# Polynomial-sketch attention followed by a sigmoid-gated feed-forward layer: other pieces for turning the first weight blocks into float32

## The chip, the cores and the metric

The kernel runs on one core of one Trainium2 chip. The metric is the device time of one execution in microseconds (us), lower is better. A difference under about 0.2% (0.6 us here) is not told from no change.

## What is computed

```
q, k, v: (4 batches, 4 heads, 1088 tokens, 32);  S1, S2: (8, 32)
phi(x) = outer product of S1 x and S2 x, flattened to 64 features
num = phi(q) @ (phi(k)^T v)      den = phi(q) . sum(phi(k)) + 1e-6
x = (num / den), heads side by side: 4352 tokens x 128
gate = sigmoid(x @ w_gate)       val = x @ w_val        # 128 x 1536 each
out = (gate * val) @ w_out                              # 1536 x 128
```

S1, S2 and the three weight matrices arrive as float64. The kernel gets their bits as pairs of 32-bit integers and makes float32 of them itself; the text calls this *narrowing*.

## The kernel before

**Feed-forward.** The 1536 hidden columns are 12 blocks of 128 (`NJ`), the 4352 tokens are chunks of 512. `w1` (line 345) computes one block of one chunk: two products into PSUM, gate and val (`wave`, line 357), which I call W0 to W11 in the first chunk; ScalarE takes the sigmoid of the gate (`sg`, line 365), and VectorE multiplies by val (`glu`, line 381). `w2` (line 307) multiplies that by the block's `w_out` and adds it up in PSUM (`moeout`, line 314) over the 12 blocks. A float32 product shows as two matmul instructions, so a `w1` is four and a `w2` two. `slot(group, n)` (line 395) issues n such steps in the order: `glu` of the last wave, `w2` of the wave before that, then the next `w1`.

**Attention** is issued between these steps by hand. For the first batch (batch 0) it comes in two parts of the queries, 512 and 576 columns (`q_chk`): part 0 must be done before W0, part 1 is done during chunk 0. For part 1, `turn_q(0, 1)` transposes the queries on VectorE (line 436), `qcomp` (line 593) multiplies them by the sketch (`cqps`, line 602), ScalarE copies the result out and sends it to DRAM, SyncE's queue brings it back spread over the partitions (`qp`, `bq`, line 627), `qmult` (line 653) multiplies the two on VectorE, and then `dn` (line 834) makes `dps` and `nps` on TensorE. Their result is divided on VectorE (lines 878 to 886), and this is what the second token chunk needs. Then batch 1 begins: `turn_k(1)`, `turn_q(1, 0)`, `turn_q(1, 1)` on VectorE, and `kps` and `cqps` on TensorE.

**Order.** The schedule is manual: on TensorE, VectorE, ScalarE and GpSimd instructions run in the order in which the program issues them. SyncE's queue issues its transfers in program order too.

**Narrowing** (`narrow`, line 83) is a generator with these steps for a part of the weights:

- step 0: GpSimd clamps the high words (`cap`, line 97), ScalarE scales the low words (`tail`, line 101);
- step 1: two VectorE instructions build the result's bits (`head`, line 105 from `cap`, and line 109 from `cap` and `head`);
- step 2: ScalarE squares `cap` (`square`, line 117, into a PSUM bank or in place in SBUF), GpSimd adds `tail` to `head` (line 118);
- step 3: VectorE writes the float32 part of `w_sb` from `square` and `head` (line 127).

`cap`, `tail` and `head` rotate over 6, 5 and 3 buffers. The parts are: gate and val of block 0; gate and val of block 1; `w_out` of blocks 0 and 1 together (these three are 256 wide, `narrow_01`); then for each block 2 to 11 gate, val and `w_out` together (384 wide, `narrow_w`). `w1` issues their steps inside the slots of chunk 0, after the sigmoid (lines 366 to 376). Blocks 10 and 11 keep `square` in SBUF, the others in PSUM.

**Loads.** Line 155 loads gate and val, line 168 `w_out` of two blocks at a time, all from SyncE's queue.

Of the kernel before, what the change touches and what calls it, by code (L numbers as in the profile page):

```python
# [8 lines left out]
F32 = mybir.dt.float32  # L9
I32 = mybir.dt.int32  # L10
# [10 lines left out]
def kernel(  # L21
# [30 lines left out]
    const = ctx.enter_context(tc.tile_pool(name="const", bufs=1))  # L52
    ld = ctx.enter_context(tc.tile_pool(name="ld", bufs=1))
    sbA = ctx.enter_context(tc.tile_pool(name="sbA", bufs=2))
    raw = ctx.enter_context(tc.tile_pool(name="raw", bufs=NJ // 2))
    sbN = ctx.enter_context(tc.tile_pool(name="sbN", bufs=1))
    sbG = ctx.enter_context(tc.tile_pool(name="sbG", bufs=6))

# [24 lines left out]
    def narrow(out, bits, eng, bank=None, copies=None):  # L83

        p, n, m = bits.shape[:3]
        lo, hi = bits[:, :, :, 0].bitcast(U32), bits[:, :, :, 1]

        def tmp(dt, tag, bufs):
            return sbN.tile([P, 3, P], dt, tag=tag, name=tag, bufs=bufs)[:p, :n, :m]

        cap, tail = tmp(I32, "cap", 6), tmp(I32, "tail", 5)
        eng.tensor_scalar(  # L97
            out=cap.bitcast(F32), in0=hi.bitcast(F32), scalar1=122880.0, scalar2=-122880.0,
            op0=ALU.min, op1=ALU.max,
        )  # L100
        nc.scalar.activation(out=tail, in_=lo, func=ACTF.Copy, scale=2.0**-29)  # L101
        yield

        head = tmp(I32, "head", 3)
        nc.vector.tensor_scalar(  # L105
            out=head, in0=cap, scalar1=3, scalar2=0x3FFFFFF8,
            op0=ALU.logical_shift_left, op1=ALU.bitwise_and,
        )
        nc.vector.scalar_tensor_tensor(  # L109
            out=head, in0=cap, scalar=-0x40000000, in1=head, op0=ALU.bitwise_and, op1=ALU.bitwise_or  # L110
        )
        yield
        square = cap.bitcast(F32)
        if bank:
            square = pso.tile([P, 512], F32, tag=bank, name="square")[:, : n * m]
            square = square.rearrange("p (n m) -> p n m", n=n)
        nc.scalar.activation(out=square, in_=cap.bitcast(F32), func=ACTF.Square)  # L117
        nc.gpsimd.tensor_tensor(out=head, in0=head, in1=tail, op=ALU.add)  # L118
        yield

        head = head.bitcast(F32)
        if copies:
            square, head = (
                bass.AP(tensor=x.tensor, offset=x.offset, ap=[list(x.ap[0]), [0, copies], [1, m]])
                for x in (square, head)
            )
        nc.vector.scalar_tensor_tensor(  # L127
            out=out, in0=square, scalar=1.265625 * 2.0**-30, in1=head, op0=ALU.is_ge, op1=MUL
        )
        yield  # L130
# [11 lines left out]
                nc.sync.dma_start(out=rows, in_=s_)  # L142


    w_sb = const.tile([P, 3, NJ, P], F32, tag="w_sb", name="w_sb")
    w_in = {}

    def load_w_in(j0, j1):
        cs = slice(j0 * P, j1 * P)
        n, jj = divmod(j0, 2)  # L150
        if wide and jj == 0:
            w_in[n] = raw.tile([P, 3, 2, P, 2], I32, tag="w_in", name="w_in")
        for i, src in enumerate((moe_w_gate, moe_w_val)):
            if wide:
                nc.sync.dma_start(  # L155
                    out=w_in[n][:, i, jj : jj + j1 - j0].rearrange("p j m w -> p (j m w)"),
                    in_=src[:, cs].bitcast(I32),
                )
            else:
                nc.sync.dma_start(  # L160
                    out=w_sb[:, i, j0:j1].rearrange("p j m -> p (j m)"), in_=src[:, cs]
                )

    def load_w_out(n):
        j0, j1 = 2 * n, 2 * n + 2
        cs = slice(j0 * P, j1 * P)
        src = moe_w_out[cs, :].bitcast(I32) if wide else moe_w_out[cs, :]
        nc.sync.dma_start(
            out=w_in[n][:, 2].rearrange("p j m w -> p j (m w)") if wide else w_sb[:, 2, j0:j1],
            in_=src.rearrange("(j p) m -> p j m", p=P),  # L170
        )

    narrowing = {}

    def narrow_w(j, step):
        if not 0 <= j < NJ:
            return
        n, jj = divmod(j, 2)
        if wide:
            if step == 0:  # L180
                narrowing[j] = narrow(
                    w_sb[:, :, j, :], w_in[n][:, :, jj], nc.gpsimd, "acc1" if j < NJ - 2 else None
                )
            next(narrowing[j])


    def narrow_01(part, step):
        if wide:
            if step == 0:
                i = (slice(0, 2), part) if part < 2 else (2, slice(0, 2))  # L190
                narrowing["01", part] = narrow(
                    w_sb[:, i[0], i[1]],
                    w_in[0][:, i[0], i[1]],
                    nc.gpsimd,
                    "acc0" if part else "acc1",
                )
            next(narrowing["01", part])


    def load_rows(src, b, t, parts=((0, T, nc.sync),)):  # L200
# [42 lines left out]
    load_w_in(0, 1)  # L243
    v_t[0] = load_v(0)
    load_w_in(1, 2)
    load_w_out(0)
    load_rows(q, 0, q_t[0], ((T0, T, nc.sync),))
    for n in range(1, NJ // 2):
        load_w_in(2 * n, 2 * n + 2)
        load_w_out(n)  # L250


    def warm(*cols):
# [53 lines left out]
    def w2(ci, j0, jn, g):  # L307
# [4 lines left out]
        for jj in range(jn):  # L312
            j = j0 + jj
            nc.tensor.matmul(  # L314
                out=moe["acc"][:, :tw],
                lhsT=w_sb[:, 2, j, :],
                rhs=g[:, jj, :tw],
                start=(j == 0),
                stop=(j == NJ - 1),
            )  # L320
        if j0 + jn == NJ:
# [6 lines left out]
            while c < t0 + tw:  # L328
# [13 lines left out]
                    )  # L342
                c += n * 32

    def w1():

        ci = moe["ci"]
        t0, tw = tok_chk[ci]
        jn = TCH // tw
        j0 = moe["w"] * jn  # L350
        wv = psm.tile([P, 2, TCH], F32, tag="wave", name="wave")

        tp = tw // 2 if ci == 0 and j0 == 0 else tw
        for o in range(0, tw, tp):
            for which in range(2):
                for jj in range(jn):
                    nc.tensor.matmul(  # L357
                        out=wv[:, which, jj * tw + o : jj * tw + o + tp],
                        lhsT=w_sb[:, which, j0 + jj, :],
                        rhs=xT[:, t0 + o : t0 + o + tp],  # L360
                        start=True,
                        stop=True,
                    )
        sg = sbG.tile([P, TCH], F32, tag="sg", name="sg", bufs=3)
        nc.scalar.activation(out=sg, in_=wv[:, 0], func=ACTF.Sigmoid)  # L365
        if ci == 0:
            if j0 == 1:
                narrow_01(2, 3)
            if 0 < j0 < NJ - 2:
                narrow_w(j0 + 1, 3)  # L370
            narrow_w(j0 + 2, 1)
            narrow_w(j0 + 2, 2)
            if j0 < 3:
                narrow_w(j0 + 3, 0)
            if j0 > 1:
                narrow_w(j0 + 4, 0)


        def glu():
            g = sbG.tile([P, TCH], F32, tag="g", name="g")  # L380
            nc.vector.tensor_tensor(out=g, in0=wv[:, 1], in1=sg, op=MUL)  # L381
            moe["todo"].append((ci, j0, jn, g.rearrange("p (j t) -> p j t", j=jn)))

        moe["gate"] = glu
        moe["w"] += 1
        if j0 + jn == NJ:
            moe["ci"] += 1
            moe["w"] = 0
# [38 lines left out]
            in_=k_t[b][:, t0:t1].rearrange("p t d -> p (t d)"),  # L427
        )

    def turn_q(b, n):  # L430
        if b >= B:
            return
        if n == 0:
            qT_of[b] = sbA.tile([P, TP, 2, 32], F32, tag="qT", name="qT", bufs=1)
        t0, tn = q_chk[n]
        nc.vector.transpose(  # L436
            out=qT_of[b][:, t0 : t0 + tn].rearrange("p t c s -> p (t c s)"),
            in_=q_t[b][:, 2 * t0 : 2 * (t0 + tn)].rearrange("p t d -> p (t d)"),
# [211 lines left out]
                        in_=bass.AP(tensor=d0.tensor, offset=offset, ap=[[8 * W1, 32]] + run),  # L650
                    )

    def qmult(b, n):
        q0 = half(QP[b], n)
        nc.vector.tensor_tensor(out=q0, in0=q0, in1=half(BQ[b], n), op=MUL)  # L655

    def kv0(j_list):
        if 0 not in KVZ:
# [34 lines left out]
            )  # L693

    def kvd(b):
        KVD[b] = sbA.tile([P, 2, 2, F], F32, tag="kvd", name="kvd")
        k0 = KVZ[b][:, : 2 * F]
        n = 2 if b > 0 else 1
        nc.scalar.copy(
# [211 lines left out]

    if wide:
        steps = narrow(s4, s_in, nc.vector, copies=4)
        for _ in range(3):
            next(steps)
    turn_k(0, 0, KBASE[2] + 1)
    if wide:
# [51 lines left out]
    mult10 = ab(None, (0, 1, 0), (psm, "wave"))  # L969
    for pi in range(2):  # L970
        outer(0, pi, NJK - 1, NJK, eng=nc.gpsimd)
    for part in range(2):
        narrow_01(part, 0)
    spread_z()
    warm(512)
    for pi in range(2):
# [6 lines left out]
    def rest(turn, rc, dT):  # L983
# [8 lines left out]
        narrow_01(0, 1)  # L992
        narrow_01(0, 2)
        ndt(0)

    divide = dn(0, 0, rest)
    warm(256)

    def head1():
        narrow_01(1, 1)  # L1000
        narrow_01(0, 3)
        narrow_01(1, 2)
        narrow_01(2, 0)
        narrow_w(2, 0)

    divide((0, 4), (4, 8), between=head1)
    narrow_01(1, 3)
    narrow_01(2, 1)
    narrow_01(2, 2)

    slot(None, 1)
    cq = {}
# [33 lines left out]
        kv(b, ZS[b])  # L1046
        kvd(b)

    slot(None, 1)
    turn_q(0, 1)  # L1050
    slot(None, 1)
    slot(q01, 6)
    qmult(0, 1)
    load_kq(1)
    slot(None, 1)
    slot(lambda: part01(lambda: narrow_w(NJ - 1, 3)), 1)
    slot(last01, 1)
    v_t[1] = load_v(1)
    for b in range(1, B):
# [60 lines left out]
```

## Time and profile before

| | us |
|---|---|
| median of 6 runs | 303.46 |
| lowest and highest | 303.32 and 303.99 |
| the profiled execution | 303.41 |
| its span, first to last instruction | 301.6 |
| mean granted TensorE clock | 0.999 of full speed |
| chunk 0, from the start of W0 to the start of its last `w2` | 15.01 to 51.13 |
| steady distance from one wave to the next in chunk 0 | 2.57 or 2.58 |

Times inside the execution are counted from the start of the span. A `timeline` line gives start, duration, engine, line, operation, output and inputs, shape; in brackets the engine's idle time before it and what ended it. The `PE` rows have modelled ends, so that a row can overlap the next one on the same engine.

### The profile page before, as it was taken

The page shows a single profiled execution, that of the slowest core. Times are in us where ns is not written, and L with a number is a line of the kernel's source. Part 1 is how long each engine was busy: PE and PEld are TensorE (multiplying, and loading weights), DVE is VectorE, ACT ScalarE, POOL GpSimd, SP SyncE. Part 2 cuts the span into 40 slices and gives each one's busy share as a digit, 9 for nine tenths or more (in the row PEclk, how much of TensorE's full clock was granted, in tenths as well). Part 3 has the DMA queues.
Part 4 walks back from the last instruction along what each step waited for, and adds up shares of the span by engine and source line. Part 5 has one row for each costly group of instructions (what it writes and reads, how often), then busy time and mean ns, then how long its engine had stood idle before and what let it go on. Part 6 is the DMA issues. An engine that isn't in the chain of part 4 may idle for free.

```text
span 301.6 us, 3642 instructions
## 1 busy us (share of the span) xinstructions
PE 294.5 (98%) x1363; PEld 137.2 (45%) x1363; DVE 154.7 (51%) x268; ACT 80.6 (27%) x150; POOL 33.0 (11%) x62
## 2 busy tenths in 40 slices
PE   8899999999999999999999999999999999999994
PEld 3444434453444444434444445344444444444683
DVE  6997789764635545383365444932232223222331
ACT  3556532222122222212232222122222222222220
POOL 1465550410000400000004000000000000000000
PEclk9999999999999999999999999999999999999999
DMA  7994340896011491360016900200020000100011
GB/s 222 348 339 112 93 141 9 200 238 181 39 17 18 139 228 30 71 193 0 0 28 162 223 17 2 36 2 0 0 33 2 0 0 12 25 0 0 9 28 19
DMA packets 30546, 24.24 MB, mean 80 GB/s; under 512 B 20480, under 2 KB 25728, under 8 KB 30528
## 3 DMA queue, kind: packets, MB, share of 16 engines
q1 hardware_dynamic: 27024, 16.15, 20.4%
q0 software_dynamic: 2592, 7.08, 10.2%
q10 hardware_dynamic: 912, 0.77, 1.0%
q8 instruction: 11, 0.18, 0.2%
q14 instruction: 7, 0.06, 0.1%
HBM read 20.73 MB, written 3.26 MB: 80 GB/s over the span
## 4 chain that ended last, share of the span: by engine, by line
PE 84%; DMA 6%; DVE 4%; POOL 2%; SPq 1%; issue 1%; ACT 0%; POOLq 0%; DVEq 0%
PE wave L357 52%; PE moeout L314 27%; DMA w_in<-in_moe_w_out_dram 2%; POOL head L118 2%; DMA kq<-in_q_dram 2%; PE nps L861 1%; DMA v<-in_v_dram 1%; DMA w_in<-in_moe_w_val_dram 1%; PE kvz L677 1%; DVE w_sb L127 1%; DVE head L109 1%; DVE qp L655 1%; DVE head L105 1%; PE kps L456 1%; SPq L155 0%
## 5 line engine op out<-in xcount | busy, mean ns | idle before, releaser
L357 PE MATMUL wave<-xT,w_sb 128*128 128x512 f32 (+1 forms) x436 | 191.6, 565 | 0.0
L381 DVE TENSOR_TENSOR g<-wave,sg 128x512 f32<-128x512 f32 x102 | 70.3, 689 | 131.0 <-ACT sg L365 130.7
L357 PEld LDWEIGHTS wave<-xT,w_sb 128*128 128x128 f32 x436 | 82.9, 190 | 93.0 <-issue 85.7
L365 ACT ACTIVATE sg<-wave 128x512 f32<-128x512 f32 x102 | 60.9, 597 | 197.8 <-PE wave L357 197.8
L314 PE MATMUL moeout<-g,w_sb 128*128 128x512 f32 (+1 forms) x216 | 105.2, 575 | 0.3 <-DVE w_sb L127 0.3
L314 PEld LDWEIGHTS moeout<-g,w_sb 128*128 128x128 f32 x216 | 39.9, 190 | 44.7 <-issue 39.1
L118 POOL TENSOR_TENSOR head<-head,tail 128x384 int32<-128x384 int32 (+2 forms) x14 | 13.4, 954 | 18.0 <-DVE head L109 14.9
L627 POOL DMA_DIRECT2D qp<-dq x6 | 3.5, 583 | 106.2 <-DMA dq<-cq 106.2
L535 DVE TENSOR_TENSOR kp<-kab 128x1152 f32<-128x1152 f32 (+2 forms) x10 | 10.5, 1070 | 0.0
L655 DVE TENSOR_TENSOR qp<-qp,bq 128x1152 f32<-128x1152 f32 (+1 forms) x7 | 9.0, 1288 | 0.0
L109 DVE SCALAR_TENSOR_TENSOR head<-cap,head 128x384 int32<-128x384 int32 (+2 forms) x14 | 7.5, 535 | 0.5
L127 DVE SCALAR_TENSOR_TENSOR w_sb<-square,head 128x384 f32<-128x384 f32 (+1 forms) x11 | 5.7, 518 | 3.9 <-POOL head L118 3.9
L258 PE MATMUL warm<-const-float32-1.0 128*128 128x512 f32 (+1 forms) x12 | 6.4, 653 | 0.8 <-PEq L1104 0.8
L324 DVE STREAM_TRANSPOSE o_sb<-moeout 128x512 f32<-128x512 f32 (+1 forms) x9 | 6.1, 679 | 1.4 <-PE moeout L314 1.3
L101 ACT ACTIVATE tail<-w_in 128x384 int32<-128x384 uint32 (+1 forms) x13 | 6.5, 522 | 0.9 <-DMA w_in<-in_moe_w_gate_dram 0.9
L627 POOL DMA_DIRECT2D bq<-dq x12 | 6.7, 574 | 0.5 <-issue 0.4
L97 POOL TENSOR_SCALAR cap<-w_in 128x384 f32<-128x384 f32 (+1 forms) x13 | 6.5, 505 | 0.0
L886 DVE TENSOR_TENSOR xT<-nps,rb 128x576 f32<-128x576 f32 (+2 forms) x9 | 5.9, 660 | 0.5
L861 PE MATMUL nps<-qp,nd 64*32 64x256 f32 (+1 forms) x128 | 5.5, 402 | 0.5 <-ACT nd L741 0.4
L436 DVE STREAM_TRANSPOSE qT<-kq 128x512 f32<-128x512 f32 (+1 forms) x8 | 5.7, 716 | 0.0
L117 ACT ACTIVATE square<-cap 128x384 f32<-128x384 f32 (+1 forms) x11 | 5.1, 463 | 1.9 <-DVE w_sb L127 1.7
L425 DVE STREAM_TRANSPOSE kT<-kq 128x1088 f32<-128x1088 f32 (+2 forms) x5 | 5.3, 1069 | 0.0
(89 smaller groups left out, 85.4 us busy)
## 6 DMA issues: line engine op xcount, KB each, us to landing
qp<-dq POOLq DMA_DIRECT2D x6, 576.0 KB, 7.5
bq<-dq POOLq DMA_DIRECT2D x12, 288.0 KB, 9.6
v<-in_v_dram SPq DMA_DIRECT2D x16, 144.0 KB, 4.3
kq<-in_k_dram SPq DMA_DIRECT2D x3, 544.0 KB, 4.2
kq<-in_q_dram SPq DMA_DIRECT2D x3, 544.0 KB, 5.2
w_in<-in_moe_w_out_dram SPq DMA_DIRECT2D x6, 256.0 KB, 6.2
w_in<-in_moe_w_gate_dram SPq DMA_DIRECT2D x5, 256.0 KB, 5.6
w_in<-in_moe_w_val_dram SPq DMA_DIRECT2D x5, 256.0 KB, 6.1
```

The lines of the kernel that those rows point to most:

```text
L97: eng.tensor_scalar(out=cap.bitcast(F32), in0=hi.bitcast(F32), scalar1=122880.0, scalar2=-122880.0, op0=ALU.min, op1=ALU.max,)
L109: nc.vector.scalar_tensor_tensor(out=head, in0=cap, scalar=-0x40000000, in1=head, op0=ALU.bitwise_and, op1=ALU.bitwise_or)
L118: nc.gpsimd.tensor_tensor(out=head, in0=head, in1=tail, op=ALU.add)
L127: nc.vector.scalar_tensor_tensor(out=out, in0=square, scalar=1.265625 * 2.0**-30, in1=head, op0=ALU.is_ge, op1=MUL)
L314: nc.tensor.matmul(out=moe["acc"][:, :tw], lhsT=w_sb[:, 2, j, :], rhs=g[:, jj, :tw], start=(j == 0), stop=(j == NJ - 1),)
L357: nc.tensor.matmul(out=wv[:, which, jj * tw + o : jj * tw + o + tp], lhsT=w_sb[:, which, j0 + jj, :], rhs=xT[:, t0 + o : t0 + o + tp], sta ...
L365: nc.scalar.activation(out=sg, in_=wv[:, 0], func=ACTF.Sigmoid)
L381: nc.vector.tensor_tensor(out=g, in0=wv[:, 1], in1=sg, op=MUL)
L535: eng.tensor_tensor(out=KP[b][:, pi, j0:j1].rearrange("p j m (i l) -> p (j m) i l", i=R), in0=bass.AP(tensor=a0.tensor, offset=a0.offset, ...
L627: get.dma_start(out=t[64 * c : 64 * c + 64 if i else P, n * H * W1 : (n + 1) * H * W1], in_=bass.AP(tensor=d0.tensor, offset=d0.offset, ap ...
L655: nc.vector.tensor_tensor(out=q0, in0=q0, in1=half(BQ[b], n), op=MUL)
L861: nc.tensor.matmul(out=t[32 * h : 32 * h + 32, c, :w], lhsT=ND[b][rows, 32 * h : 32 * h + 32], rhs=half(QP[b], n)[rows, 2 * (h % 2) + h // ...
```

## The change

- Gate and val of block 2 become a part of their own (256 wide, after those of blocks 0 and 1), and `w_out` of block 0 and of block 1 become parts of their own (128 wide).
- From then on the part j (3 to 11) is gate and val of block j with `w_out` of block j - 1 (384 wide); a part 12 is `w_out` of block 11 alone (128 wide). There are 15 parts of the weights instead of 13, over the same 36 x 128 columns.
- `narrow` gets one more yield, between its two `head` instructions, so that its steps are numbered 0 to 4.
- `square` stays in SBUF for parts 10, 11, 12 and for `w_out` of block 1.
- `turn_q(0, 1)`, one transposition of 576 columns before the second `glu`, becomes two of 320 and 256, issued inside the slots of W2 and W3 (`between`). The group `q01` (`cqps` and what follows) moves from before W3 to before W4.
- `w_out` is loaded as blocks 0, 1, 2, then (3, 4), (5, 6), (7, 8), (9, 10), 11: eight transfers instead of six.
- The tile `kvd` has one buffer instead of two; the raw words of each block pair have a tile of their own name; `w_sb` is laid out flat with one spare block, and `qmult` gets arguments that no call uses.

```diff
     def load_w_out(j0, j1):
+        src = moe_w_out[j0 * P : j1 * P, :]
+        to = w_sb[:, 2 * NJ + 1 + j0 : 2 * NJ + 1 + j1]
+        if wide:
+            n, jj = divmod(j0 + 1, 2)
+            to = w_in[n][:, 2 if n < NJ // 2 else 0, jj : jj + j1 - j0]
...
+    def narrow_w(part, *steps):
+        for step in steps if part in places else ():
             if step == 0:
+                at, bits, bank = places[part]
+                narrowing[part] = narrow(w_sb[:, at], bits, nc.gpsimd, bank)
+            next(narrowing[part])
+
+    places = {}
+    for j in range(NJ if wide else 0):
+        bits = w_in[j // 2][:, :, j % 2]
+        if j < 3:
+            at = slice(j, j + NJ + 1, NJ)
+            places["gv", j] = at, bits[:, :2], f"acc{1 - j % 2}"
+        else:
+            at = slice(j, j + 2 * NJ + 1, NJ)
+            places[j] = at, bits, "acc1" if j < NJ - 2 else None
+    if wide:
+        for j, bank in enumerate(("acc0", None)):
+            places["out", j] = (
+                slice(2 * NJ + 1 + j, 2 * NJ + 2 + j), w_in[j][:, 2, 1 - j : 2 - j], bank
+            )
+        places[NJ] = slice(3 * NJ, 3 * NJ + 1), w_in[NJ // 2][:, 0], None
...
-    load_w_out(0)
+    load_w_out(0, 1)
+    load_w_out(1, 2)
     load_rows(q, 0, q_t[0], ((T0, T, nc.sync),))
     for n in range(1, NJ // 2):
         load_w_in(2 * n, 2 * n + 2)
-        load_w_out(n)
+        if n == 1:
+            load_w_out(2, 3)
+        else:
+            load_w_out(2 * n - 1, 2 * n + 1)
+    load_w_out(NJ - 1, NJ)
...
         if ci == 0:
-            if j0 == 1:
-                narrow_01(2, 3)
-            if 0 < j0 < NJ - 2:
-                narrow_w(j0 + 1, 3)
-            narrow_w(j0 + 2, 1)
-            narrow_w(j0 + 2, 2)
-            if j0 < 3:
-                narrow_w(j0 + 3, 0)
-            if j0 > 1:
-                narrow_w(j0 + 4, 0)
+            if j0 == 0:
+                narrow_w(("gv", 2), 1, 2, 3)
+                narrow_w(("out", 0), 4)
+                narrow_w(3, 0)
+            elif j0 == 1:
+                narrow_w(("gv", 2), 4)
+                narrow_w(("out", 1), 1, 2, 3)
+                narrow_w(3, 1, 2)
+                narrow_w(("out", 1), 4)
+                narrow_w(3, 3)
+                narrow_w(4, 0)
+            else:
+                if j0 in between:
+                    between[j0]()
+                if j0 != NJ - 2:
+                    narrow_w(j0 + 1, 4)
+                narrow_w(j0 + 2, 1, 2, 3)
+                if j0 <= 6:
+                    narrow_w(j0 + 3, 0)
+                if j0 >= 6:
+                    narrow_w(j0 + 4, 0)
...
     def head1():
-        narrow_01(1, 1)
-        narrow_01(0, 3)
-        narrow_01(1, 2)
-        narrow_01(2, 0)
-        narrow_w(2, 0)
+        narrow_w(("gv", 1), 1, 2)
+        narrow_w(("gv", 0), 4)
+        narrow_w(("gv", 1), 3)
+        narrow_w(("out", 0), 0)
+        narrow_w(("gv", 2), 0)
+        narrow_w(("out", 1), 0)
     divide((0, 4), (4, 8), between=head1)
-    narrow_01(1, 3)
-    narrow_01(2, 1)
-    narrow_01(2, 2)
+    narrow_w(("gv", 1), 4)
+    narrow_w(("out", 0), 1, 2, 3)
...
-    slot(None, 1)
-    turn_q(0, 1)
-    slot(None, 1)
-    slot(q01, 6)
+    between.update({2: lambda: turn_q(0, 1, 0, 5), 3: lambda: turn_q(0, 1, 5)})
+    slot(None, 3)
+    slot(q01, 5)
     qmult(0, 1)
     load_kq(1)
     slot(None, 1)
-    slot(lambda: part01(lambda: narrow_w(NJ - 1, 3)), 1)
+    slot(lambda: part01(lambda: narrow_w(NJ - 1, 4)), 1)
     slot(last01, 1)
```

More of the change, by code (lines that the diff above doesn't have):

```diff
@@ L54 @@
     sbA = ctx.enter_context(tc.tile_pool(name="sbA", bufs=2))
-    raw = ctx.enter_context(tc.tile_pool(name="raw", bufs=NJ // 2))
+    raw = ctx.enter_context(tc.tile_pool(name="raw", bufs=1))
     sbN = ctx.enter_context(tc.tile_pool(name="sbN", bufs=1))
@@ L108, in narrow @@
         )
+        yield
         nc.vector.scalar_tensor_tensor(
@@ L142, in load_s @@
                 nc.sync.dma_start(out=rows, in_=s_)
-    w_sb = const.tile([P, 3, NJ, P], F32, tag="w_sb", name="w_sb")
-    w_in = {}
+    w_sb = const.tile([P, 3 * NJ + 1, P], F32, tag="w_sb", name="w_sb")
+    w_in = []
+    for n in range(NJ // 2 + 1 if wide else 0):
+        shape = [3, 2] if n < NJ // 2 else [1, 1]
+        w_in.append(raw.tile([P] + shape + [P, 2], I32, tag=f"w_in{n}", name="w_in"))
     def load_w_in(j0, j1):
@@ L150, in load_w_in @@
         n, jj = divmod(j0, 2)
-        if wide and jj == 0:
-            w_in[n] = raw.tile([P, 3, 2, P, 2], I32, tag="w_in", name="w_in")
         for i, src in enumerate((moe_w_gate, moe_w_val)):
@@ L160, in load_w_in @@
                 nc.sync.dma_start(
-                    out=w_sb[:, i, j0:j1].rearrange("p j m -> p (j m)"), in_=src[:, cs]
-                )
[L164 to L171, printed above, removed]
@@ L173 @@
-    narrowing = {}
[L175 to L179, printed above, removed]
-            if step == 0:
[L181 to L197, printed above, removed]
+                    out=w_sb[:, i * NJ + j0 : i * NJ + j1].rearrange("p j m -> p (j m)"),
@@ new lines, in load_w_in, with load_w_out @@
+                    in_=src[:, cs],
+                )
+    def load_w_out(j0, j1):
+        src = moe_w_out[j0 * P : j1 * P, :]
[3 more added lines that the diff above has]
+            to = w_in[n][:, 2 if n < NJ // 2 else 0, jj : jj + j1 - j0]
+            to = to.rearrange("p j m w -> p j (m w)")
+            src = src.bitcast(I32)
+        nc.sync.dma_start(out=to, in_=src.rearrange("(j p) m -> p j m", p=P))
+    narrowing = {}
@@ L315, in w2 @@
                 out=moe["acc"][:, :tw],
-                lhsT=w_sb[:, 2, j, :],
+                lhsT=w_sb[:, 2 * NJ + 1 + j, :],
                 rhs=g[:, jj, :tw],
@@ L343, in w2 @@
                 c += n * 32
+    between = {}
     def w1():
@@ L358, in w1 @@
                         out=wv[:, which, jj * tw + o : jj * tw + o + tp],
-                        lhsT=w_sb[:, which, j0 + jj, :],
+                        lhsT=w_sb[:, which * NJ + j0 + jj, :],
                         rhs=xT[:, t0 + o : t0 + o + tp],
@@ L428, in turn_k, with turn_q @@
         )
-    def turn_q(b, n):
+    def turn_q(b, n, u0=0, u1=None):
         if b >= B:
@@ L435, in turn_q @@
         t0, tn = q_chk[n]
+        t0, tn = t0 + u0, (u1 or tn) - u0
         nc.vector.transpose(
@@ L651, in spread, with qmult @@
                     )
-    def qmult(b, n):
-        q0 = half(QP[b], n)
-        nc.vector.tensor_tensor(out=q0, in0=q0, in1=half(BQ[b], n), op=MUL)
+    def qmult(b, n, h0=0, h1=H):
+        q0, b0 = half(QP[b], n)[:, h0:h1], half(BQ[b], n)[:, h0:h1]
+        nc.vector.tensor_tensor(out=q0, in0=q0, in1=b0, op=MUL)
     def kv0(j_list):
@@ L695, in kvd @@
     def kvd(b):
-        KVD[b] = sbA.tile([P, 2, 2, F], F32, tag="kvd", name="kvd")
+        KVD[b] = sbA.tile([P, 2, 2, F], F32, tag="kvd", name="kvd", bufs=1)
         k0 = KVZ[b][:, : 2 * F]
@@ L913 @@
         steps = narrow(s4, s_in, nc.vector, copies=4)
-        for _ in range(3):
+        for _ in range(4):
             next(steps)
@@ L971 @@
         outer(0, pi, NJK - 1, NJK, eng=nc.gpsimd)
-    for part in range(2):
-        narrow_01(part, 0)
+    narrow_w(("gv", 0), 0)
+    narrow_w(("gv", 1), 0)
     spread_z()
@@ L991, in rest @@
         kvd(0)
-        narrow_01(0, 1)
-        narrow_01(0, 2)
+        narrow_w(("gv", 0), 1, 2, 3)
         ndt(0)
```

## The prediction, made blind

> **What bounds it.** First the page's busy times:
>
> ```profile
> span 301.6 us, 3642 instructions
> ...
> PE 294.5 (98%) x1363; PEld 137.2 (45%) x1363; DVE 154.7 (51%) x268; ACT 80.6 (27%) x150; POOL 33.0 (11%) x62
> ```
>
> TensorE (PE) is the bound; no product is added or removed, so only its gaps can change. The busy times by stretch (columns: length, then PE, PEld, DVE, ACT, POOL busy with counts, clock, DMA share, GB/s) show which gaps the edits can reach:
>
> ```profile
> 15.00:23.40 8.40, 8.06 (x29) 3.82 (x29) 7.96 (x18) 4.86 (x11) 4.61 (x8) 1.00 1.06 323
> 23.40:40.58 17.18, 17.18 (x41) 7.40 (x39) 13.34 (x25) 9.64 (x20) 10.40 (x14) 1.00 0.32 83
> 42.10:51.10 9.00, 9.00 (x58) 3.84 (x50) 8.35 (x16) 2.31 (x4) 0.99 (x1) 1.00 0.32 115
> ```
>
> VectorE (DVE) is nearly full in the first and third. The timeline of PE tells what the first gap costs:
>
> ```profile
> 15.01 3.71 PE L357 MATMUL wave<-xT,w_sb 128*128 128x256 f32 x12
> 19.05 1.12 PE L314 MATMUL moeout<-g,w_sb 128*128 128x512 f32 x2 [0.34 <-DVE w_sb L127]
> 20.02 1.88 PE L357 MATMUL wave<-xT,w_sb 128*128 128x512 f32 x4
> 21.82 0.69 PE L602 MATMUL cqps<-qT,skq 64*32 64x288 f32 x8
> ```
>
> In steady state a wave takes 1.72 and a w2 0.86. sg of W0 starts at 17.04 and of W1 at 18.75, elsewhere 0.2 after the wave's end, so W1 ends at 18.56 and w2(0) is 0.49 late. It ends at 19.91, W2 starts at 20.02: 0.11 more. At most 0.60 can be won here. The timeline of all engines says why:
>
> ```profile
> 16.33 0.42 DVE L109 SCALAR_TENSOR_TENSOR head<-cap,head 128x256 int32<-128x256 int32 x1
> ...
> 16.93 0.72 POOL L118 TENSOR_TENSOR head<-head,tail 128x256 int32<-128x256 int32 x1 [1.04 <-DVE head L109]
> ...
> 17.06 1.01 DVE L109 SCALAR_TENSOR_TENSOR head<-cap,head 128x384 int32<-128x384 int32 x1
> ...
> 17.99 0.68 DVE L381 TENSOR_TENSOR g<-wave,sg 128x512 f32<-128x512 f32 x1
> ...
> 18.59 0.41 DVE L127 SCALAR_TENSOR_TENSOR w_sb<-square,head 128x256 f32<-128x256 f32 x1
> ```
>
> The final step of w_out (18.59) stands behind everything DVE does for block 2 and behind glu. And L109 took 1.01 instead of 0.56: it ended 0.42 after GpSimd's (POOL's) addition, as if it had waited for it.
>
> Then the chain of waits:
>
> ```profile
> 37.03 1.01 POOL head L118
> ...
> 38.07 0.56 DVE w_sb L127
> 38.62 0.28 DVE head L105
> ...
> 38.93 0.06 DVE head L109
> ...
> 39.40 1.36 DVE qp L655
> ...
> 40.81 0.69 PE dps L841 x8
> ```
>
> From part 3 on, addition, final step, L105, L109, next addition form a ring of 2.62 per wave against PE's 2.576. It sets when qmult (L655) runs, and PE, done with W9 at 40.58, waits for it. So a gain at 19 us survives only if the ring comes earlier too.
>
> **The parts, costed.** 128-wide steps aren't in the trace. Bounds are the 128x256 rows above and the 16-partition rows of S (L105 0.17, L109 0.18, L127 0.24, L118 0.24). I extend the lines through 384 and 256 wide to 128, as the S rows have 16 partitions: L105 0.19, L109 0.28, L127 0.27, L118 0.46, cap 0.27. An instruction behind an independent one starts 0.08 before that ends (16.33 + 0.42 against 16.67), behind one that it needs 0.04 after; L118 starts 0.18 after L109's end. So the three DVE steps of a 128-wide part take 0.22 + 0.20 + 0.20 = 0.62 of DVE (0.39 to 1.0 by the bounds).
>
> Head. Up to gate and val of block 1 (15.68) nothing changes. Then:
> - w_out 0: L105 16.01, L109 16.23 to 16.51, addition 16.69 to 17.15. Block 2's L109 meets that addition and ends 0.30 after it, 17.45. Final w_out 0 from 17.37 to 17.65; glu of W0 waits for sg (17.64) and runs to 18.35. **w2(0) can start at 18.56**, W2 at 19.42 (its final step ends 18.79), ending at 21.14.
> - w_out 1: L105 waits for the clamp of part 3 (18.31 to 18.84); L109 to 19.27; addition from 19.47 to 19.93. Part 3's L105 from 19.19, its L109 is due at 19.58 and again waits for the addition, to 20.35. Final w_out 1 20.27 to 20.55, glu of W1 to 21.15: w2(1) at 21.20, 0.06 late.
> - The first piece of q, 320 columns: 0.50, between 0.44 (256) and 0.70 (512); the two pieces cost 0.94 against 0.77. Final of part 3 21.55 to 22.11, W3 22.16 (0.1 late), L109 of part 4 to 22.97, its addition at **23.14 instead of 23.56**. glu, second piece to 23.93, cqps 23.99, w2(2) at about 24.7, W4 at 25.58 instead of 25.98: PE is 0.40 ahead.
>
> Ring. Before, two clamps in one slot (24.52, 1.03 long) delayed an L105 to 0.68 and that turn of the ring to 2.98. The change has two clamps in the slot of W6 instead: the same 0.33 once, only later. So qmult comes 0.42 + 0.36 - 0.33 = 0.45 early, 38.95 to 40.30, and dps at 40.36 instead of 40.81; W9's end at 40.18 hides. **Lead: 0.45.**
>
> Tail. After qmult DVE has no idle to speak of until batch 1's queries are turned:
>
> ```profile
> 48.83 1.36 DVE L436 STREAM_TRANSPOSE qT<-kq 128x512 f32<-128x512 f32 x2
> ...
> 50.51 0.69 PE L602 MATMUL cqps<-qT,skq 64*32 64x288 f32 x16
> ```
>
> Part 12 adds its 0.62 in front of them. Its clamp follows POOL's addition for part 10 at once, and part 10's final step (41.65, both inputs in SBUF) then costs 0.08 more (0 to 0.27). The transposition ends at 50.19 + 0.70 less the lead; cqps follows 0.06 later: 50.95 less the lead, against 50.51 now. kps before it covers 0.26 of this, **0.44 is paid**. Product, glu and w2 up to there keep over 0.4 of slack. After cqps batch 1 is anchored on PE and shifts with it.
>
> Sum: 0.44 - 0.45 = -0.01, that is **303.40 against the profiled 303.41**; the median lies 0.05 higher, so 303.45, rounded to 303.5.
>
> Costed at nothing:
> - Two more issues on SyncE's queue, some 0.65 each by their spacing (6.09, 6.74, 7.38). Block 2's words land up to 0.6 later, hidden until DVE asks at 16.4; batch 1's v goes out at 19 instead of 18, and the next transfer on that queue waits until 27.08. Without that cover, 1.3. The bytes are the same; nothing moves past POOL's queue.
> - q01 a wave later: ScalarE's copy at about 25.9 instead of 24.03, the fetch at 28.9 instead of 27.08. DMA activity of that fetch ends near 33.8, then 35.7; qmult asks at 38.95. Cover 3.2. ScalarE's copy and send (0.63 + 0.50) fit before sg of W4 at 27.5.
> - kvd with one buffer: its readers are done long before the next copy (12.76, then 65.86).
> - ScalarE's two more tails and squares, about 0.3 each: ScalarE idles 1.1 before every sg.
>
> A rule is weighed here, apart from the sum. The Trainium skill, "SBUF — State Buffer", section "Who interferes with whom", says that VectorE and GpSimd share a port pair as an exclusive lock, also when a VectorE instruction has two SBUF inputs and GpSimd reads SBUF. The rows at 17.06 and 25.09 agree; no row shows a final step with square in SBUF meeting GpSimd. By the rule w_out 1's final step would be open to it where a PSUM square is not (24.59 ran 0.56 beside a clamp), and lose up to one addition, 1.0: +1.0 by the rule where the rows give -0.01.
>
> **Rivals.**
> 1. *Slower, 304.5.* Place: slot of W1. If part 3's L109 (due 19.58) gets in before w_out 1's addition (due 19.44), it ends at 20.15, the addition runs 20.15 to 20.6, and part 3's addition follows at once. w_out 1's final step then comes behind a POOL instruction of 1.0 with both inputs in SBUF: by the row at 17.06 as bound it waits until 21.57, glu ends at 22.33, part 4's addition starts at 24.24, 0.68 later than before. 0.44 + 0.68 = 1.12: 304.5. It decides from a delay of 0.14 at the first addition. Against it: at 16.93 and 17.06 the same two steps had 0.13 between them and POOL won. For it: three such meetings stand in a row.
> 2. *Faster, 302.8.* Part 12 costs nothing at the tail and the lead reaches PE's own limit, 0.60 and the 0.15 that dps waited: 302.7 to 302.8. For: PE has these gaps. Against: the DVE rows up to 50.19 stand shoulder to shoulder, and with no POOL meeting at all I get a lead of 0.66, thus only 303.2.
> 3. *It does not do what it says:* w2(0) stays late because glu, not w_out, comes last. glu's bound is sg, 17.64, so under 0.1 speaks for it; the ring's lead would still hold: 303.5.
>
> **Numbers.** Forecast with rival 3, within 0.2%: 0.69. Rival 1 and its lesser forms: 0.19. Rival 2: 0.12. The forecast's own range, from a lead of 0.66 (no meeting) to 0.1 (both dearer by 0.17) and 0.2 either way for the 128-wide steps, is 303.0 to 304.0. For 8 in 10 it is drawn out to 302.8 and 304.3. These chances are also those of faster, same and slower by 0.2% (0.6 us), about what a measurement of this kernel tells from no change.
>
> **What would show it.** w2(0) at 18.5 to 18.7, W2 at 19.4; L109 of part 3 longer than 0.7; part 4's addition near 23.1; dps near 40.4; at batch 1 a PE gap of 0.4 before cqps, ended by qT. Wrong if part 4's addition starts after 23.6, if the final step of w_out 1 lasts over 0.6, or if cqps follows kps with no gap.

## The result and the profile after

| | before | changed |
|---|---|---|
| median of all runs, us | 303.54 (69 runs) | 304.13 (33 runs) |
| ratio, 95% interval | | 1.0019 (1.0014 to 1.0024) |
| a second comparison, with runs of its own | 303.60 (35) | 304.08 (12), ratio 1.0015 (1.0005 to 1.0026) |
| the profiled execution, its span | 303.41, 301.6 | 303.74, 302.0 |

The changed kernel is 0.15 to 0.2% slower, 0.46 to 0.58 us. That is within the 0.2% that were called no change, close to their upper end: both intervals lie above 1, and both reach beyond 1.002. (The ratios leave out two runs with a granted clock of 0.989: 308.54 us for the changed kernel and 308.17 for the kernel before.)

In the changed kernel the lines have other numbers: the clamp is L97 and L105 stays, L109 is L110, the addition L119, the final step L128, a wave L374, w2 L329, glu L410, qmult L685, cqps L632. First the head of its page:

```profile
span 302.0 us, 3668 instructions
...
PE 295.2 (98%) x1363; PEld 137.0 (45%) x1363; DVE 155.6 (52%) x275; ACT 81.3 (27%) x154; POOL 33.7 (11%) x66
```

The matmuls are the same 1363. VectorE has seven instructions more, six for two more parts and one for the second piece of q; GpSimd and ScalarE have four more each. The busy times by stretch of the changed kernel, in the same three stretches and columns as before:

```profile
15.00:23.40 8.40, 8.40 (x23) 4.15 (x24) 8.15 (x21) 4.97 (x11) 4.78 (x10) 1.00 1.05 321
23.40:40.58 17.18, 17.03 (x50) 6.96 (x52) 13.70 (x27) 10.00 (x21) 10.42 (x14) 1.00 0.29 83
42.10:51.10 9.00, 8.63 (x50) 3.44 (x48) 8.85 (x19) 2.62 (x5) 1.45 (x2) 1.00 0.28 109
```

In the first stretch TensorE's 0.34 us of idle time are gone. In the third, where it had none, it now has 0.37, and VectorE is busy for 8.85 of 9.00 instead of 8.35. The timeline of TensorE in the changed kernel shows both places:

```profile
14.91 3.71 PE L374 MATMUL wave<-xT,w_sb 128*128 128x256 f32 x12
18.46 1.02 PE L329 MATMUL moeout<-g,w_sb 128*128 128x512 f32 x2
19.32 1.88 PE L374 MATMUL wave<-xT,w_sb 128*128 128x512 f32 x4
...
40.46 0.69 PE L871 MATMUL dps<-qp,zb 128*32 128x288 f32 x8
...
50.74 0.72 PE L632 MATMUL cqps<-qT,skq 64*32 64x288 f32 x16 [0.37 <-DVE qT L466]
```

W0 starts at 14.91 here and at 15.01 before. The change moves some transfers and narrowing steps ahead of W0, but they cost nothing there: from the first `kps` of batch 0 (5.92 here, 6.01 before) to W0 it takes 8.99 and 9.00. Counted from W0, w2(0) comes after 3.55 instead of 4.04, dps after 25.55 instead of 25.80, cqps after 35.83 instead of 35.50. From there to the last `w2` (295.27 and 295.01) the two timelines keep their distance within 0.03. So all of it happens between W0 and cqps of batch 1, and distances from W0 are used from here on.

The engines around w2(0) and w2(1) in the changed kernel:

```profile
16.63 0.45 POOL L119 TENSOR_TENSOR head<-head,tail 128x128 int32<-128x128 int32 x1 [0.83 <-DVE head L110]
16.69 0.67 DVE L110 SCALAR_TENSOR_TENSOR head<-cap,head 128x256 int32<-128x256 int32 x1
17.29 0.28 DVE L128 SCALAR_TENSOR_TENSOR w_sb<-square,head 128x128 f32<-128x128 f32 x1
...
19.36 0.46 POOL L119 TENSOR_TENSOR head<-head,tail 128x128 int32<-128x128 int32 x1 [0.59 <-ACT sg L382]
...
19.49 0.74 DVE L110 SCALAR_TENSOR_TENSOR head<-cap,head 128x384 int32<-128x384 int32 x1
20.16 0.28 DVE L128 SCALAR_TENSOR_TENSOR w_sb<-cap,head 128x128 f32<-128x128 f32 x1
```

The final step of w_out 0 (17.29) now stands ahead of glu, and twice L110 is stretched by an addition of GpSimd that began just before it (0.67 instead of some 0.42, 0.74 instead of 0.56). Then one turn of the ring, from one 384-wide addition to the next:

```profile
25.73 1.00 POOL L119 TENSOR_TENSOR head<-head,tail 128x384 int32<-128x384 int32 x1 [1.16 <-ACT tail L101]
26.70 0.53 POOL L97 TENSOR_SCALAR cap<-w_in 128x384 f32<-128x384 f32 x1
26.76 0.56 DVE L128 SCALAR_TENSOR_TENSOR w_sb<-square,head 128x384 f32<-128x384 f32 x1 [0.61 <-POOL head L119]
...
27.26 0.36 DVE L105 TENSOR_SCALAR head<-cap 128x384 int32<-128x384 int32 x1
27.66 0.56 DVE L110 SCALAR_TENSOR_TENSOR head<-cap,head 128x384 int32<-128x384 int32 x1
28.39 1.00 POOL L119 TENSOR_TENSOR head<-head,tail 128x384 int32<-128x384 int32 x1 [1.16 <-DVE head L110]
```

28.39 - 25.73 = 2.66, not 2.62. The clamp ends at 27.23, and L105 starts 0.03 later: with a lead of three parts, the clamp that runs behind the addition is the one that L105 needs next. The kernel before clamps four parts ahead from W2 on, the changed kernel only from W6. (The releasers named for the additions differ from turn to turn; each starts 0.17 after the end of L110, as in the kernel before.) Last, VectorE ahead of cqps:

```profile
41.24 0.34 POOL L97 TENSOR_SCALAR cap<-w_in 128x128 f32<-128x128 f32 x1
41.30 0.70 DVE L128 SCALAR_TENSOR_TENSOR w_sb<-cap,head 128x384 f32<-128x384 f32 x1 [0.29 <-POOL head L119]
...
45.55 0.18 DVE L105 TENSOR_SCALAR head<-cap 128x128 int32<-128x128 int32 x1
45.76 0.29 DVE L110 SCALAR_TENSOR_TENSOR head<-cap,head 128x128 int32<-128x128 int32 x1
...
47.24 0.28 DVE L128 SCALAR_TENSOR_TENSOR w_sb<-cap,head 128x128 f32<-128x128 f32 x1
...
49.24 1.35 DVE L466 STREAM_TRANSPOSE qT<-kq 128x512 f32<-128x512 f32 x2
```

Part 12's three steps, and part 10's final step, which takes 0.70 instead of 0.56 beside part 12's clamp, stand in front of the transpositions. Those end at 50.59, cqps follows at 50.74.

### The profile page after: what moved, and what is told of

It reads as the page before. It is cut to its first block, busy times and chain, and to the rows that moved or that the text cites. A ratio compares the mean times of both kernels' runs of the same rounds, so it can differ in the third digit from the quotient of the medians.

```text
span 302.0 us, 3668 instructions
## 1 busy us (share of the span) xinstructions
PE 295.2 (98%) x1363; PEld 137.0 (45%) x1363; DVE 155.6 (52%) x275; ACT 81.3 (27%) x154; POOL 33.7 (11%) x66
## 4 chain that ended last, share of the span: by engine, by line
PE 88%; DVE 5%; issue 2%; POOL 2%; ACT 1%; DMA 1%; SPq 0%; DVEq 0%; POOLq 0%
PE wave L374 54%; PE moeout L329 28%; PE nps L891 1%; POOL head L119 1%; PE kvz L707 1%; DMA s_in<-in_S_dram 1%; PE cqps L632 1%; DVE kT L454 1%; DVE w_sb L128 1%; DVE head L110 1%; PE deni L841 0%; PE kvz L693 0%; PE kps L486 0%; DVE qT L466 0%; DVE qp L685 0%
## 5 line engine op out<-in xcount | busy, mean ns | idle before, releaser
L374 PE MATMUL wave<-xT,w_sb 128*128 128x512 f32 (+1 forms) x436 | 191.7, 566 | 0.0
L410 DVE TENSOR_TENSOR g<-wave,sg 128x512 f32<-128x512 f32 x102 | 70.3, 689 | 130.5 <-ACT sg L382 130.1
L374 PEld LDWEIGHTS wave<-xT,w_sb 128*128 128x128 f32 x436 | 82.7, 190 | 93.2 <-issue 86.2
L329 PE MATMUL moeout<-g,w_sb 128*128 128x512 f32 (+1 forms) x216 | 105.2, 575 | 0.0
L329 PEld LDWEIGHTS moeout<-g,w_sb 128*128 128x128 f32 x216 | 39.8, 190 | 44.4 <-issue 39.3
L119 POOL TENSOR_TENSOR head<-head,tail 128x384 int32<-128x384 int32 (+3 forms) x16 | 13.7, 857 | 19.8 <-DVE head L110 11.7
L685 DVE TENSOR_TENSOR qp<-qp,bq 128x1152 f32<-128x1152 f32 (+1 forms) x7 | 9.0, 1288 | 0.0
L110 DVE SCALAR_TENSOR_TENSOR head<-cap,head 128x384 int32<-128x384 int32 (+3 forms) x16 | 7.8, 487 | 0.6
L128 DVE SCALAR_TENSOR_TENSOR w_sb<-square,head 128x384 f32<-128x384 f32 (+2 forms) x11 | 5.4, 494 | 3.3 <-POOL head L119 3.3
L101 ACT ACTIVATE tail<-w_in 128x384 int32<-128x384 uint32 (+2 forms) x15 | 6.8, 477 | 0.7 <-DMA w_in<-in_moe_w_gate_dram 0.7
L97 POOL TENSOR_SCALAR cap<-w_in 128x384 f32<-128x384 f32 (+2 forms) x15 | 6.8, 464 | 0.0
L466 DVE STREAM_TRANSPOSE qT<-kq 128x512 f32<-128x512 f32 (+3 forms) x9 | 5.8, 654 | 0.0
L105 DVE TENSOR_SCALAR head<-cap 128x384 int32<-128x384 int32 (+3 forms) x16 | 5.3, 332 | 0.0
```

Of the source, the lines that this page charges most:

```text
L110: nc.vector.scalar_tensor_tensor(out=head, in0=cap, scalar=-0x40000000, in1=head, op0=ALU.bitwise_and, op1=ALU.bitwise_or)
L128: nc.vector.scalar_tensor_tensor(out=out, in0=square, scalar=1.265625 * 2.0**-30, in1=head, op0=ALU.is_ge, op1=MUL)
L329: nc.tensor.matmul(out=moe["acc"][:, :tw], lhsT=w_sb[:, 2 * NJ + 1 + j, :], rhs=g[:, jj, :tw], start=(j == 0), stop=(j == NJ - 1),)
L374: nc.tensor.matmul(out=wv[:, which, jj * tw + o : jj * tw + o + tp], lhsT=w_sb[:, which * NJ + j0 + jj, :], rhs=xT[:, t0 + o : t0 + o + tp ...
L685: nc.vector.tensor_tensor(out=q0, in0=q0, in1=b0, op=MUL)
```

## The experiments

The theory: between 15 and 51 us the end is set by VectorE. A loss in the ring of VectorE and GpSimd, or in VectorE's almost unbroken row from qmult to the transpositions of batch 1's queries, reaches cqps, while TensorE's own gaps in the head count only if the ring gains with them. The first four runs undo one thing each.

**1. The final step of part 12 behind the transpositions.**

```diff
-                if j0 != NJ - 2:
+                if j0 < NJ - 2:
                     narrow_w(j0 + 1, 4)
...
         turn_q(b, 1)
+        if b == 1:
+            narrow_w(NJ, 4)
         slot(lambda: begin(b), 1)
```

> Only the final VectorE step of part 12 (w_out of block 11) is moved behind the transpositions of batch 1's queries. Theory (VectorE's unbroken row from qmult to those transpositions sets when batch 1's cqps runs, and so the end): the row gets 0.20 us shorter, cqps at about 50.5 instead of 50.74, the time 0.2 us under the changed kernel, about 0.4 us over the kernel before. Rival (the loss lies elsewhere, in the loads or in the head): no change against the changed kernel, 0.6 us over the kernel before.

Measured: ratio to the kernel before 1.0011 (1.0002 to 1.0020), 0.33 us. cqps 35.61 after W0, 0.22 earlier than in the changed kernel (the theory: 0.20).

**2. Clamps four parts ahead from W2.**

```diff
-                if j0 <= 6:
+                if j0 == 2:
                     narrow_w(j0 + 3, 0)
-                if j0 >= 6:
+                if j0 >= 2:
                     narrow_w(j0 + 4, 0)
```

> The clamps run four parts ahead from the slot of W2 on (two clamps there) and not only from W6. Theory (with a lead of three the clamp, 0.53 us behind the addition, stands in the ring of addition, final step, L105, L109 and makes a turn 2.66 instead of 2.62 us): turns of 2.62 us, one turn of about 2.98 at the two clamps, qmult at about 38.9 instead of 39.06, cqps and the time 0.15 us under the changed kernel. Rival (the longer turns come from something else, such as the loads that run meanwhile): turns stay 2.66 us and the time stays.

Measured: 1.0011 (1.0003 to 1.0020); cqps 35.68, 0.15 earlier. The timeline of this kernel, a turn of its ring (one part later than the turn shown above):

```profile
29.23 1.00 POOL L119 TENSOR_TENSOR head<-head,tail 128x384 int32<-128x384 int32 x1 [1.13 <-DVE head L110]
30.20 0.53 POOL L97 TENSOR_SCALAR cap<-w_in 128x384 f32<-128x384 f32 x1
30.27 0.56 DVE L128 SCALAR_TENSOR_TENSOR w_sb<-square,head 128x384 f32<-128x384 f32 x1 [0.61 <-POOL head L119]
30.74 0.35 DVE L105 TENSOR_SCALAR head<-cap 128x384 int32<-128x384 int32 x1
...
31.86 1.00 POOL L119 TENSOR_TENSOR head<-head,tail 128x384 int32<-128x384 int32 x1 [1.13 <-DVE head L110]
```

A turn is 2.63 again: L105 follows the final step by 0.47 (0.50 above), with the same clamp beside it, which it no longer needs. The clamp was in the ring.

**3. Without part 12.**

```diff
-        places[NJ] = slice(3 * NJ, 3 * NJ + 1), w_in[NJ // 2][:, 0], None
+        nc.gpsimd.memset(w_sb[:, 3 * NJ], 0.0)
```

> Part 12 is left out: w_out of block 11 is not narrowed and is zero, so its share of the output is missing. Theory (part 12's three VectorE steps, 0.62 us, and the 0.14 us by which its clamp lengthens part 10's final step, are what makes cqps late): the gap before cqps goes, cqps follows kps at about 50.15, the time is 0.55 to 0.6 us under the changed kernel and equal to the kernel before within 0.1, or up to 0.2 us under it. Rival (the loss is in the head or in the ring): under 0.1 us of change.

Measured: 0.9994 (0.9985 to 1.0003). cqps 35.28 after W0, 0.55 earlier than in the changed kernel and 0.22 earlier than before:

```profile
49.90 0.72 PE L486 MATMUL kps<-kT,sk 64*32 64x288 f32 x16
...
50.41 0.69 PE L632 MATMUL cqps<-qT,skq 64*32 64x288 f32 x16
```

cqps follows kps after 0.51, as in the kernel before. The whole of what the head gains is 0.22 us, and the tail loses 0.55.

**4. The queries in one piece, before the second glu.**

```diff
-    between.update({2: lambda: turn_q(0, 1, 0, 5), 3: lambda: turn_q(0, 1, 5)})
-    slot(None, 3)
+    slot(None, 1)
+    turn_q(0, 1)
+    slot(None, 2)
```

> The queries of batch 0's part 1 are turned in one piece again, before the second glu, the rest as in the changed kernel. Theory (the ring and VectorE's row set the end, not TensorE's gaps in the head): w2(1) comes 0.7 us later (21.8 instead of 21.09), but part 4's addition only 0.2 us later, and the time is 0.2 us over the changed kernel. Rival (TensorE's gaps in the head pass straight to the end): 0.6 to 0.7 us over the changed kernel.

Measured: 1.0024 (1.0016 to 1.0032). w2(1) starts 0.66 later than in the changed kernel (6.84 instead of 6.18 after W0), part 4's addition only 0.12 later, cqps 0.11 later. A delay of 0.66 on TensorE in the head shrinks to 0.33 at dps (25.88, behind W9) and to 0.11 at cqps: the rival, that such gaps pass straight to the end, is out. By these distances, turning q in two pieces is worth 0.11 us, or 0.03 against the second execution of the changed kernel (below): no more than that kernel's own scatter.

**5. Part 12 out of the way.** Its steps move behind the transpositions, and w2 of block 11 one wave later.

```diff
-                if j0 != NJ - 2:
+                if j0 < NJ - 2:
                     narrow_w(j0 + 1, 4)
-                narrow_w(j0 + 2, 1, 2, 3)
+                    narrow_w(j0 + 2, 1, 2, 3)
...
-            lag = 3 if last else 2
+            lag = 3 if last or (moe["ci"], moe["w"]) == (1, 1) else 2
...
         turn_q(b, 1)
+        if b == 1:
+            narrow_w(NJ, 1, 2, 3)
         slot(lambda: begin(b), 1)
+        if b == 1:
+            narrow_w(NJ, 4)
```

> Part 12's VectorE steps are moved behind the transpositions of batch 1's queries, its final step behind kab, and the last w2 of chunk 0 (block 11) one wave later, so that it does not wait for them. Theory (part 12 in front of those transpositions is what makes cqps late): cqps follows kps without a gap, 35.3 us after the start of W0 (changed kernel 35.8, kernel before 35.5); the time is like that of the kernel without part 12, 0.1 to 0.2 us under the kernel before. Rival (the work only moves the wait: part 12 is then late for the later w2, or kab is late): the gap comes back as a wait of that w2, the time 0.4 us or more over the kernel before.

Measured: 1.0007 (0.9996 to 1.0017), between the two expectations. cqps comes at 35.26 as the theory had it, but the third wave of chunk 1 at 39.77 (39.66 before). The timeline shows the new wait, and it is neither of the two that the rival named:

```profile
49.81 0.60 ACT L382 ACTIVATE sg<-wave 128x512 f32<-128x512 f32 x1 [1.92 <-PE wave L374]
...
50.22 0.69 PE L632 MATMUL cqps<-qT,skq 64*32 64x288 f32 x16
50.44 0.69 DVE L410 TENSOR_TENSOR g<-wave,sg 128x512 f32<-128x512 f32 x1
...
51.19 1.98 PE L374 MATMUL wave<-xT,w_sb 128*128 128x512 f32 x4 [0.28 <-DVE g L410]
```

The two wave buffers are shared by the waves and cqps. The next wave needs the buffer that glu frees at 51.13; the w2 that stood here used to cover that.

**6. Both: part 12 out of the way and the clamps four ahead** (the edits of 5 and 2).

> Both: part 12 behind as in the run before it, and the clamps four parts ahead from W2 on. Theory (the two losses add, up to the limit that TensorE's own W9 sets for dps, 25.3 us after W0): dps 25.4 and cqps 35.1 us after W0, the time 0.3 to 0.4 us under the kernel before. Rival (with part 12 out of the way nothing on VectorE counts any more): as the run before it, within 0.05.

Measured: 1.0001 (0.9988 to 1.0013). dps 25.42 and cqps 35.12 after W0, as expected, so the two losses do add. But the wait for the wave buffer stays (0.28, at 51.77), the third wave of chunk 1 comes at 39.63 instead of 39.66, and the time is that of the kernel before. The interval alone reaches down to 0.36 us below it; the distance shows that the 0.3 to 0.4 were not won.

**7. Clamps three parts ahead to the end.**

```diff
-                if j0 <= 6:
+                if j0 <= 9:
                     narrow_w(j0 + 3, 0)
-                if j0 >= 6:
-                    narrow_w(j0 + 4, 0)
```

> The clamps stay three parts ahead to the end: no slot with two clamps, but the clamps of parts 11 and 12 now follow the additions of parts 10 and 11 at once, where the final steps read square from SBUF. Theory (a GpSimd instruction and a VectorE instruction with two SBUF inputs keep each other out): qmult 0.28 us earlier, part 10's final step 0.9 us long instead of 0.70 and part 11's 0.7 instead of 0.56, the time within 0.1 us of the changed kernel. Rival (only the two clamps in one slot count, the final steps are not held): the final steps stay at 0.56 to 0.7 us and the time is 0.25 us under the changed kernel.

Measured: 1.0021 (1.0010 to 1.0032). qmult 0.27 earlier; cqps 0.06 to 0.14 later than in the two executions of the changed kernel. The final steps of parts 10 and 11 in this kernel's timeline, 0.56 each in the kernel before:

```profile
41.09 0.67 POOL L97 TENSOR_SCALAR cap<-w_in 128x384 f32<-128x384 f32 x1
41.15 1.02 DVE L128 SCALAR_TENSOR_TENSOR w_sb<-cap,head 128x384 f32<-128x384 f32 x1 [0.30 <-POOL head L119]
...
44.17 0.30 POOL L97 TENSOR_SCALAR cap<-w_in 128x128 f32<-128x128 f32 x1
44.24 0.64 DVE L128 SCALAR_TENSOR_TENSOR w_sb<-cap,head 128x384 f32<-128x384 f32 x1
```

Both end 0.41 after the clamp that began just before them, as if they had waited for it. Together they take 0.40 longer than in the changed kernel, which outweighs the 0.27 won at qmult. With square in PSUM the same step ran 0.56 beside a clamp of the same size (26.76 above). So by these rows it is the second input in SBUF that lets GpSimd hold the step.

**8 and 9. Each of the two kernels once more.**

> The changed kernel once more, as it is, for a second execution in profile. From the first one: cqps 35.8 us after the start of W0, 0.33 us more than before. If the start of W0 itself scatters by some tenths of a us between executions (14.91 to 15.47 so far) while that distance stays within 0.05, then the scatter belongs to the stage ahead of W0, which the change does not touch, and the distance is the effect. If the distance scatters too, VectorE and GpSimd do not always meet in the same order.

> The kernel before once more, as it is, for a second execution in profile. Expected: cqps of batch 1 35.50 us and the third wave of chunk 1 39.66 us after the start of W0, each within 0.1, whatever the start of W0 itself is (15.01 in the first one).

| distance from W0, us | start of W0 | dps | cqps | third wave of chunk 1 |
|---|---|---|---|---|
| before | 15.01 | 25.80 | 35.50 | 39.66 |
| before again | 14.93 | 25.79 | 35.49 | 39.65 |
| changed | 14.91 | 25.55 | 35.83 | 40.01 |
| changed again | 15.23 | 25.64 | 35.91 | 40.10 |
| 1 final step late | 15.15 | 25.53 | 35.61 | 39.80 |
| 2 clamps four ahead | 15.47 | 25.41 | 35.68 | 39.87 |
| 3 no part 12 | 15.13 | 25.58 | 35.28 | 39.44 |
| 4 q in one piece | 15.02 | 25.88 | 35.94 | 40.13 |
| 5 part 12 away | 14.96 | 25.56 | 35.26 | 39.77 |
| 6 both | 15.68 | 25.42 | 35.12 | 39.63 |
| 7 clamps three ahead | 15.02 | 25.32 | 35.97 | 40.16 |
| 10 gap filled | 15.51 | 25.41 | 35.55 | 39.73 |

The start of W0 scatters over 0.8 us. All of it arises ahead of the first `kps` of batch 0, which comes 8.99 or 9.00 before W0 in every one of these executions: most of it is in TensorE's `warm` products there (the last two of them took 0.70 in eight executions and 0.78 to 1.22 in the four with the latest W0), for a reason that no run shows. In the two kernels that were profiled twice, the distances repeat within 0.09. The order in which VectorE and GpSimd meet was the same in both executions of the changed kernel.

**10. Filling the gap of 5 and 6.** w2 of block 10 goes between kps and cqps, part 12's first steps behind glu. The edits are against the kernel of run 6:

```diff
-            lag = 3 if last or (moe["ci"], moe["w"]) == (1, 1) else 2
+            lag = 3 if last or (moe["ci"], moe["w"]) in ((1, 0), (1, 1)) else 2
...
         glu()
+        if b == 1:
+            narrow_w(NJ, 1, 2, 3)
         kps(b)
+        if b == 1:
+            w2(*moe["todo"].pop(0))
...
         turn_q(b, 1)
-        if b == 1:
-            narrow_w(NJ, 1, 2, 3)
```

> As the run with both edits, but w2 of block 10 is held back too and put between kps and cqps of batch 1, and part 12's first steps stand behind the glu of chunk 1's first wave: work for TensorE in the time in which it waited 0.35 us for that glu. Theory (TensorE then has no gap from W11 to the third wave of chunk 1): that wave starts 39.45 to 39.5 us after W0 (kernel before 39.66, both edits 39.63, changed kernel 40.0), the time is 0.15 to 0.25 us under the kernel before. Rival (the transpositions of batch 1's queries come too late for the earlier cqps): a gap before cqps of 0.2 us or more, no gain over the run with both edits.

Measured: 1.0005 (0.9995 to 1.0015); the third wave of chunk 1 at 39.73. Neither expectation was met: no gap of 0.2 us is left, and yet nothing is gained.

```profile
49.36 0.71 PE L486 MATMUL kps<-kT,sk 64*32 64x288 f32 x16
50.00 1.13 PE L329 MATMUL moeout<-g,w_sb 128*128 128x512 f32 x2
51.06 0.72 PE L632 MATMUL cqps<-qT,skq 64*32 64x288 f32 x16
51.70 1.98 PE L374 MATMUL wave<-xT,w_sb 128*128 128x512 f32 x4
```

From kps to the next wave it takes 2.34 (before: 2.09, from 50.00 to 52.09) for the same products. From start to start, kps takes 0.64 instead of 0.51 when cqps does not follow it, and w2 1.06 between the two instead of 0.86 between waves. The new order cost what the gap of 0.28 was worth, or a little more (39.73 against 39.63 in run 6). No version was clearly faster than the kernel before.

## Why the prediction was right, point by point

The time was forecast as 303.45, no change (-0.01 us), and came out at 304.13 against 303.54. "No change within 0.2%" held, but narrowly: the interval of the ratio reaches to 0.24%, and 304.13 lies above the forecast's own range (303.0 to 304.0), inside the wider one (to 304.3). The places of gain and loss were right, and the signs named came within 0.1 (among them dps at 40.46 and a gap of 0.37 before cqps, ended by qT). But one wait in the ring was overlooked and the cover at the tail was taken too large, and both cost time. That the loss stayed within the 0.2% was partly luck.

- **Head.** Right. w2(0), forecast at 18.56, came at 18.46 (with W0 0.10 early), W2 at 19.32 (19.42), the final step of w_out 1 at 20.16 (20.27), part 4's addition at 23.07 (23.14). Both meetings of L109 with an addition happened as drawn, 0.67 and 0.74 long.
- **Ring.** The step that was mis-sized: the lead at qmult, taken as 0.45, was 0.24 (24.15 instead of 24.39 after W0), and 0.16 in the second execution. At part 4's addition the lead still was 0.39 of the 0.42 forecast; the rest went in the turns behind it. The prediction took a turn of 2.62 for all of them and moved only the slot with two clamps. It overlooked that the lead of the clamps is three, not four, until W6, which puts the clamp's 0.53 in place of the final step's 0.47: four turns of 2.66 instead of 2.62 (from 23.07 to 33.72), 0.16 us. Run 2 took that away and won 0.15. The two clamps in one slot cost 0.36 (a turn of 2.98 from 33.72 to 36.70) where 0.33 was forecast. The kernel before had shown the longer turn itself, where it still clamps three parts ahead:

```profile
20.90 0.99 POOL L118 TENSOR_TENSOR head<-head,tail 128x384 int32<-128x384 int32 x1 [1.17 <-ACT tail L101]
...
21.86 0.54 POOL L97 TENSOR_SCALAR cap<-w_in 128x384 f32<-128x384 f32 x1
21.93 0.56 DVE L127 SCALAR_TENSOR_TENSOR w_sb<-square,head 128x384 f32<-128x384 f32 x1
...
22.43 0.36 DVE L105 TENSOR_SCALAR head<-cap 128x384 int32<-128x384 int32 x1
...
23.56 1.00 POOL L118 TENSOR_TENSOR head<-head,tail 128x384 int32<-128x384 int32 x1 [1.16 <-ACT tail L101]
```

23.56 - 20.90 = 2.66, and L105 starts 0.03 after the clamp's end.

- **Tail.** Nearly right: 0.74 against 0.70. The three steps have 0.18, 0.29 and 0.28, part 10's final step 0.70 instead of 0.56. The cover by kps was 0.17, not 0.26, as cqps starts 0.15, not 0.06, after the transposition. 0.74 - 0.17 = 0.57 was paid, not 0.44; run 3 without part 12 measured 0.55.
- **Sum.** 0.57 - 0.24 = 0.33, the distance of the first pair of profiles (0.41 with the second execution). The comparisons say 0.46 and 0.58, both with intervals that reach down to about 0.4 or below it. In all ten comparisons with the kernel before, the time is 0.02 to 0.26 us further over it than the third wave of chunk 1 is. The start of W0 may hold some of this (15.21 on average over ten executions of the changed kernel and its variants, 14.97 over two of the kernel before), and the last output's transfers may; that was not settled.
- **Costed at nothing.** The fetch of q's products was issued from 28.78 on (28.9 forecast), and qmult followed L110 without a wait. The waits name a load once between W0 and cqps, at the addition at 20.40, but it too starts 0.17 after the end of L110 (19.49 + 0.74), so no load cost anything there. ScalarE idled less than the 1.1 said ahead of the first two sigmoids (0.57 and 0.36), which came no later for it.
- **Rival 1** (w_out 1's final step behind part 3's addition) did not happen: 20.16, 0.28 long, the addition at 20.40. Its mechanism is real, though, as run 7 shows at parts 10 and 11 (1.02 and 0.64 instead of 0.56), and part 10 of the changed kernel (0.70), GpSimd having begun 0.06 or 0.07 earlier each time. The Trainium skill, "SBUF — State Buffer", "Who interferes with whom", says that a VectorE instruction with two SBUF inputs contends with a GpSimd instruction that reads SBUF; these rows agree. The 1.0 that the prediction derived from this rule was not paid, as no GpSimd instruction ran when w_out 1's final step began.
- **Rival 2** (nothing paid at the tail, the lead up to TensorE's limit) did not happen; run 6 came nearest to it, and a wait for a wave buffer took the gain.
- **Rival 3** did not hold: w2(0) came when it was said to.

## What to carry to other kernels

A gap on the bounding engine is worth closing only if the engine that feeds it gets ahead too: here 0.6 us of gaps closed on TensorE brought qmult only 0.24 forward, and a delay of 0.66 put back there moved cqps by 0.11 at most, since VectorE and GpSimd passed work to each other in a ring of their own. When the order of a software pipeline is changed, list for each step how far ahead its inputs are made, as one part less of lead put a clamp into the ring; and look where the fixed costs of a part that is split off will land, here at the end, where the engine had almost no idle time.

## What was not expected of the hardware

- The final step with both inputs in SBUF was held by a GpSimd clamp (0.56 to 1.02, and to 0.64 and 0.70 beside shorter ones), the same step with one input in PSUM was not (0.56 beside a clamp of 0.53).
- Where products with different tiles (128*128 and 64*32 in the rows) follow one another, TensorE took some 0.1 us more at each change, without showing idle time: from start to start w2 takes 0.86 between waves, 0.96 behind cqps and 1.06 between kps and cqps, and two more changes in run 10 cost 0.25. That the tiles are the reason was not tested apart.
- The start of W0 scatters over 0.8 us between executions (14.91 to 15.68), more than the whole effect, and all of it arises ahead of the first `kps`, most of it in TensorE's `warm` products.
